# Half of g's blocks back to TensorE for tiles 4 to 9 of a fused attention, MoE and soft-MoE kernel

## The chip, the cores and the metric

One core of a Trainium2 chip runs the whole program. The metric is the device time of one execution in microseconds, the median of several; lower is better. The kernel before takes 519.07 us (3 runs, 516.73 to 519.13).

## The reference

Three layers follow each other, all in float32. The first is attention for 4 batches and 8 heads of width 64: 512 local queries see a band of 32 positions to either side and the 32 global keys, and 32 global queries see everything. The second is a dense layer pair with a leaky ReLU. The third is a soft mixture of experts with 8 experts of 4 slots.

```python
out_g = softmax(scale * q_g @ k_all.T) @ v_all
out_l = softmax([scale * q_l @ k_g.T, masked(scale * q_l @ k_l.T)]) @ [v_g, v_l]
x = concat([out_g, out_l])          # 4*544 rows of 512
h = x @ w_in                        # 512 -> 2048
g = maximum(0.01 * h, h)
x = g @ w_out                       # 2048 -> 512
logits = x @ phi                    # 512 -> 32 slots
d = softmax over rows(logits);  c = softmax over slots(logits)
slot_input = d.T @ x
slot_out[e] = maximum(slot_input[e] @ w1[e], 0) @ w2[e]
out = c @ slot_out
```

## The kernel before, in words

The 2176 rows of x are worked in 17 tiles of 128 rows (`NTT`): tiles 0 to 15 are the local queries of four batches, four tiles each, and tile 16 the global queries. The product with `w_out` is never formed per row: `pmat` holds `w_out @ phi`, so the logits come straight from g, and the product `d.T @ g` (`b_U`, into `uacc`) is multiplied by `w_out` once at the end.

For each tile t the work has two halves.

- **H(t)**, in `b_H`: for each of four blocks f of 512 features, 12 matmuls (`hp`, line 684) form h on TensorE, and ScalarE evicts them with the leaky ReLU to g (line 691).
- **L(t)**: g is needed with its features on the partitions to be multiplied by `pmat` (`b_M`, `lg`, line 735). There are two ways to turn it. In `b_L`, TensorE transposes four 128x128 blocks into a PSUM bank (`gtp`, line 721), and ScalarE or VectorE copies the bank to `gT` (line 723). In `blocks`, VectorE turns every 32x32 block in place (`gb`, line 703), and 16 copies per pair of f, of 32 partitions by 256 elements, move the blocks to their place (`g8`, line 712). The table `MOVE` says who copies: for f = 0 and 1 GpSimd alone, for f = 2 and 3 six copies on GpSimd, five on VectorE, five on ScalarE.

The logits then go through the softmax over rows, in running form: `b_D1` copies them out (`lp`, line 744), `b_D2` sums the four parts on TensorE (line 750), takes the maximum (line 754) and the exponentials (`st`, line 759, and the copy of line 760), `b_D3` transposes them back (line 795) and copies `d` (line 782), and `b_U` multiplies `d` with g (`up`, line 805) and adds to `uacc` (line 810).

`BLK` names the tiles that take the way through `blocks`: tiles 4 to 14. Tiles 0 to 3 and the last two take `b_L`.

The attention of batches 2 and 3 is recorded between the tiles: `merge` lays its steps (`a_T`: transposes of k and q, `kTp` and `qTp`, evicted by ScalarE to `kT` and `qT`; `a_S`: scores `sc`, mask and maximum `se` on VectorE, exponentials on ScalarE; `a_E`: transposes `etp`, evicted to `eT`; `a_V`: `po`) beside the items of `b_items`. All transposes of the attention and of `b_L` share two PSUM banks, `tp`.

Two things set the order on an engine. A scheduler places the recorded instructions by their order in the program and by their dependences. And `behind` wraps an item in `tc.issue_after(ms["b"])`: its TensorE instructions may not stand ahead of the last matmul of the chain of L. In `b_items`, for a tile of `BLK` the halves 4 to 7 of H(t) stand behind the chain of L(t-1) in this way; for other tiles there is no such edge.

Past line 643 a line of the changed kernel has a number higher by one.

Of the kernel before, what the change touches and what calls it, by code (L numbers as in the profile page):

```python
# [20 lines left out]
def kernel(  # L21
# [26 lines left out]
    NTT = B * NT + 1  # L48
# [13 lines left out]
    def tp(name):  # L62
        return bank("tp", name, 2)

    def hb(name):
        return bank("hb", name, 2)
# [149 lines left out]
    def part(name, dt=F32):  # L216

        if not spare:
            t = sb.tile([P, 2, 512], dt, tag="gT", name=name, bufs=2)
            spare.extend((t[:, 1], t[:, 0]))  # L220
        return spare.pop()
# [418 lines left out]
    gt = {}  # L640
    ms = {}
    seq = [(b, T) for b in range(B) for T in range(NT)] + [None]
    BLK = range(4, NTT - 2)
    MOVE = "P" * 16, "PPPPPPDDDDDAAAAA"
    gp = []

    def b_X(t):
        if seq[t] is None:
            pt = xg0.rearrange("p k t -> p (k t)")
        else:  # L650
            b, T = seq[t]
            pt = tp("xtp")
            for i in range(KD):
                nc.tensor.transpose(
                    pt[:, P * i:P * i + P],
                    xn[b][:, T, 2 * i:2 * i + 2, :].rearrange("p h d -> p (h d)"), ident,
                )
        pool, tags = (sa, ("qn", "kn")) if t == 2 else (sb, ("xh", "xl"))
        xh, xl = (pool.tile([P, KD, P], F32R, tag=g, name="x" + g, bufs=2) for g in tags)
        nc.scalar.mul(xh.rearrange("p k t -> p (k t)"), pt, WS)  # L660
        nc.vector.scalar_tensor_tensor(
            out=xl.rearrange("p k t -> p (k t)"), in0=pt, scalar=WS,
            in1=xh.rearrange("p k t -> p (k t)"), op0=ALU.mult, op1=ALU.subtract,
        )
        xt[t] = (xh, xl)
# [3 lines left out]
    def b_H(t, f, half=None):  # L669
        xh, xl = xt[t]  # L670
        if half != 1:
            if f == 0:
                gt[t] = (
                    xa.tile([P, FF], F32, tag="xn", name="gx", bufs=1) if t in (3, NTT - 1)
                    else sa.tile([P, FF], F32, tag="vw", name="g2", bufs=2) if t == 2
                    else sb.tile([P, FF], F32, tag="g", name="g", bufs=2)
                )
            hps[0] = hb("hp")
        hp = hps[0]
        w = wi[f]  # L680
        lo, hi = {None: (0, KD), 0: (0, KD // 2), 1: (KD // 2, KD)}[half]
        for k in range(lo, hi):
            for n, (a, c) in enumerate(((xh, 0), (xh, 1), (xl, 0))):
                nc.tensor.matmul(  # L684
                    hp, a[:, k, :], w[c][:, k, :],
                    start=(k == 0 and n == 0), stop=(k == KD - 1 and n == 2),
                )
        if half == 0:
            return
        gs = gt[t][:, 512 * f:512 * f + 512]  # L690
        nc.scalar.activation(out=gs, in_=hp, func=AF.Prelu, alpha=0.01)  # L691
        if t in BLK:
            blocks(t, f, gs)

    gbl = {}
# [1 line left out]
    def blocks(t, f, gs):  # L697

        if f % 2 == 0:
            gbl[0] = sb.tile([P, 2, 512], F32, tag="gT", name="gb", bufs=2)  # L700
            gbl[1] = gp[0].tile([P, 2, 4, P], F32, tag="g8", name="g8", bufs=2)
        gb, g8 = gbl[0], gbl[1]
        nc.vector.transpose(out=gb[:, f % 2], in_=gs)  # L703
        lst[t, f] = g8[:, f % 2]
        if f % 2 == 0:
            return
        src = gb.rearrange("p f (q c j) -> p (f q) c j", c=4, j=32)
        dst = g8.rearrange("p f q (a j) -> p (f q) a j", j=32)
        for n in range(16):
            a, c = n // 4, (n + n // 4) % 4  # L710
            copy = {"P": nc.gpsimd.tensor_copy, "A": nc.scalar.copy, "D": nc.vector.tensor_copy}[MOVE[f // 2][n]]
            copy(dst[32 * c:32 * c + 32, :, a], src[32 * a:32 * a + 32, :, c])  # L712
# [3 lines left out]
    def b_L(t, f, ev=None):  # L716
        g = gt[t]
        pt = tp("gtp")
        for c in range(4):
            o = 512 * f + P * c  # L720
            nc.tensor.transpose(pt[:, P * c:P * c + P], g[:, o:o + P], ident)  # L721
        gT = part("gT")
        (ev or (nc.vector.tensor_copy if f % 2 and not (t >= 6 and f in (1, 3, 9)) else nc.scalar.copy))(
            gT, pt
        )
        lst[t, f] = gT.rearrange("p (c t) -> p c t", c=4)

    def b_M(t, fs=range(NQ)):
        if 0 in fs:
            ms["M"] = bank("sm", "lg", 1)  # L730
        lg = ms["M"]
        for f in fs:
            gT = lst.pop((t, f))
            for c in range(4):
                ms["b"] = nc.tensor.matmul(  # L735
                    lg[32 * c:32 * c + 32, 0:P], pmat[:, c, f, :], gT[:, c, :],
                    start=(f == 0), stop=(f == NQ - 1), skip_group_check=True,
                ).ins
        return lg

    def b_D1(t):
        lg = b_M(t, range(2, NQ) if t in BLK else range(NQ))
        lp = sb.tile([P, 2 * P], F32, tag="lp", name="lp", bufs=1)[:, 0:P]
        nc.vector.tensor_copy(lp, lg[:, 0:P])
        ms["lg"] = lg, lp
# [28 lines left out]
    def b_D2(t):  # L774
        lg, lp = ms["lg"]
        ms["st"] = d_cols(lg[:, P:2 * P], lp)
        ms["b"] = ms["mm"]
# [15 lines left out]
    def b_D3(t):  # L793
        lg, _ = ms["lg"]
        ms["b"] = nc.tensor.transpose(lg[:, 256:384], ms["st"], ident).ins
        ms["d"] = d_rows(t, lg[:, 256:320])
# [19 lines left out]
    def b_U(t):  # L816
        u_add([(ms["d"], gt.pop(t))], t)
# [44 lines left out]

    def l_items(t):
        return ([(0.0, lambda: None), (0.6, lambda: b_M(t, range(2)))] if t in BLK else [
            (0.9, lambda: (b_L(t, 0), b_L(t, 1))),
            (0.9, lambda: (b_L(t, 2), b_L(t, 3))),
        ]) + [
            (1.3, lambda: b_D1(t)),
            (0.3, lambda: b_D2(t)),
            (0.1, lambda: b_D3(t)),  # L870
            (1.0, lambda: b_U(t)),
        ]

    def h_items(t):
        its = [(2.6, lambda f=f: b_H(t, f)) for f in range(NQ)]
        if t + 1 < NTT:
            its.insert(2, (0.5, lambda: b_X(t + 1), t + 1))
        return its

    def behind(item):  # L880
        def go():
            with tc.issue_after(ms["b"]):
                item[1]()
        return (item[0], go) + item[2:]

    def b_items(t0, t1):
        its = []
        for t in range(t0, t1):
            li = l_items(t - 1)
            h = [(1.3, lambda t=t, f=f, a=a: b_H(t, f, a)) for f in range(NQ) for a in range(2)]  # L890
            x = [(0.5, lambda t=t: b_X(t + 1), t + 1)] if t + 1 < NTT else []
            if t - 1 in BLK:
                its += h[0:2] + [li[1]] + h[2:4] + [li[2]] + x + [behind(h[4])]
                its += [li[3]] + [behind(x) for x in h[5:8]] + [li[4], li[5]]
                continue
            its += h[0:2] + [li[0]] + h[2:4] + [li[1]] + h[4:5] + x + h[5:6]
            its += [li[2], h[6], li[3], h[7], li[4], (0.0, lambda: None), li[5]]
        return its
# [19 lines left out]
    t = wp.tile([P, 4, NT, 2, D], F32, tag="w", name="qk")  # L918
# [29 lines left out]
    for t in range(3):  # L948
        b_X(t)
        b_H(t, 0)  # L950
# [28 lines left out]
    for x in l_items(2):  # L979
        x[1]()  # L980
    load_v(NP + 1)
    l0, l1 = l_items(0), l_items(1)
    merge(l0 + h3[2:] + l1, s4[-1:] + s5 + s6 + s7)
    b_X(NT)
# [342 lines left out]
```

## Time and profile before

| What | Value |
|---|---|
| median of 3 runs | 519.07 us |
| the profiled execution, its own time | 516.28 us |
| its span in the profile | 514.2 us |
| mean granted clock of TensorE | 0.962 |
| TensorE busy with matmuls | 464.5 us (90%) |
| VectorE busy | 301.2 us (59%) |
| ScalarE busy | 248.7 us (48%) |
| GpSimd busy | 181.1 us (35%) |

The span is what the instructions cover; the time has what lies around it too. Busy shares are means over stages with different limits. The weights are converted and the attention of batches 0 and 1 runs until about 205 us; tiles 4 to 9 pass through L from there to about 360 us; tiles 10 to 16 follow until 450 us, and the experts, whose weights stream in, end the program.

### The profile page before, as it was taken

To read this page: it belongs to the slowest core of one execution; us is meant where nothing else is said; L and a number is where in the kernel's file an instruction comes from. 1 tells how busy PE (TensorE), PEld (TensorE's weight loads), DVE (VectorE), ACT (ScalarE), POOL (GpSimd) and SP (SyncE) were. 2 spreads that over 40 slices of the span, in tenths; PEclk is the share of its full clock that TensorE was granted. 3 is DMA by queue.
4 is the path that set the end of the run, shared out by engine and by line. 5 is a ranking of instruction groups with operands and counts; after the bars stand their busy time and mean duration, and the time that the engine had idled before them with its cause. 6 is when DMAs were issued, how large, how long until landed. Compare 5 with 4: busy or idle time off the path is not lost.

```text
span 514.2 us, 13727 instructions
## 1 busy us (share of the span) xinstructions
PE 464.5 (90%) x5279; PEld 322.2 (63%) x5279; DVE 301.2 (59%) x996; ACT 248.7 (48%) x762; POOL 181.1 (35%) x345
## 2 busy tenths in 40 slices
PE   8976988978999989689898899999999999999994
PEld 5644766556775657456675667677777777633353
DVE  4586769759576663866766975656555541312422
ACT  4787878759654163444525473144433442300222
POOL 2066688443202015206263636516656620000000
PEclk9978899979998999879999999999999999999998
DMA  9998767799755750602480500229620059999987
GB/s 178 235 231 229 212 216 297 209 303 275 189 116 107 169 114 1 131 8 56 127 149 9 108 8 0 84 83 399 256 83 2 0 196 342 385 378 377 302 249 207
DMA packets 122397, 90.25 MB, mean 176 GB/s; under 512 B 75804, under 2 KB 101212, under 8 KB 122332
## 3 DMA queue, kind: packets, MB, share of 16 engines
q1 hardware_dynamic: 119660, 88.33, 60.2%
q10 hardware_dynamic: 2672, 1.05, 0.8%
q8 instruction: 41, 0.67, 0.6%
q14 instruction: 24, 0.20, 0.1%
HBM read 76.68 MB, written 8.65 MB: 166 GB/s over the span
## 4 chain that ended last, share of the span: by engine, by line
PE 60%; DVE 13%; ACT 7%; DMA 5%; issue 3%; POOL 2%; SPq 0%; ACTq 0%; POOLq 0%; DVEq 0%
PE hp L684 29%; PE ehp L1167 3%; PE up L805 3%; PE lg L735 3%; ACT se L452 2%; PE gtp L721 2%; PE sc L432 2%; DMA rraw<-in_moe_w_out_dram 2%; DVE se L444 2%; DMA rraw<-in_moe_w_in_dram 2%; PE po L489 2%; PE sop L1243 1%; POOL wn L259 1%; PE etp L471 1%; PE sop L1221 1%
## 5 line engine op out<-in xcount | busy, mean ns | idle before, releaser
L684 PE MATMUL hp<-wi,xxh 128*128 128x512 f32 x512 | 166.5, 407 | 7.1 <-ACT g L691 3.6
L712 POOL COPY g<-gb 32x256 f32<-32x256 f32 x242 | 97.6, 403 | 95.8 <-DVE gb L703 37.5
L684 PEld LDWEIGHTS hp<-wi,xxh 128*128 128x128 f32 x512 | 92.8, 191 | 41.2 <-issue 12.0
L684 PE MATMUL hp<-wi,xxl 128*128 128x512 f32 x256 | 101.5, 397 | 0.0
L452 ACT ACTIVATE se<-se,nmx 128x128 f32<-128x128 f32 x128 | 49.6, 390 | 24.2 <-DVE nmx L450 21.4
L691 ACT ACTIVATE g<-hp 128x512 f32<-128x512 f32 x60 | 35.7, 594 | 47.6 <-PE hp L684 46.9
L684 PEld LDWEIGHTS hp<-wi,xxl 128*128 128x128 f32 x256 | 48.7, 190 | 12.1 <-issue 0.8
L703 DVE STREAM_TRANSPOSE gb<-g 128x512 f32<-128x512 f32 x44 | 30.9, 706 | 19.4 <-ACT g L691 19.0
L200 POOL COPY vw<-vw 32x1664 f32<-32x1664 f32 x10 | 15.7, 1574 | 70.1 <-DMA vw<-in_v_g_dram 39.2
L259 POOL TENSOR_TENSOR wn<-wn,rraw 128x256 int32<-128x256 int32 x32 | 26.3, 836 | 32.6 <-DMA rraw<-in_moe_w_in_dram 23.4
L432 PE MATMUL sc<-kw,qT 64*32 64x128 f32 x1024 | 29.3, 292 | 1.1 <-issue 0.7
L444 DVE CUSTOM_DVE_ANT_0 se<-sc,mask 128x128 f32<-128x128 f32 x128 | 28.7, 282 | 1.4 <-PE sc L432 1.2
L471 PE MATMUL etp<-identr,se 128*128 128x128 f32 x128 | 23.1, 301 | 5.3 <-ACT kT L392 4.0
L259 POOL TENSOR_TENSOR wo<-wo,rraw 128x256 int32<-128x256 int32 x23 | 18.1, 800 | 25.5 <-DMA rraw<-in_moe_w_out_dram 4.5
L712 ACT COPY g<-gb 32x256 f32<-32x256 f32 x55 | 22.1, 402 | 9.2 <-DVE cs L788 4.1
L489 PE MATMUL po<-vw,eT 128*32 128x64 f32 x1024 | 24.0, 227 | 2.4 <-DMA vw<-vw 1.5
L249 ACT ACTIVATE rraw<-rraw 128x256 int32<-128x256 uint32 x55 | 23.2, 435 | 5.9 <-DMA rraw<-in_moe_w_in_dram 5.1
L432 PEld LDWEIGHTS sc<-kw,qT 64*32 64x32 f32 x1024 | 20.2, 112 | 7.7 <-issue 4.0
L403 DVE COPY kw<-kT 128x672 f32<-128x672 f32 x32 | 19.2, 638 | 9.0 <-ACT kT L392 8.8
L759 ACT ACTIVATE st<-lg,nm 128x128 f32<-128x128 f32 (+1 forms) x16 | 6.0, 373 | 38.2 <-DVE nm L758 34.5
L489 PEld LDWEIGHTS po<-vw,eT 128*32 128x32 f32 x1024 | 18.4, 113 | 9.7 <-issue 7.3
L452 ACT ACTIVATION_READ_ACCUMULATOR se<-se,nmx 128x1 f32 x128 | 24.1, 188 | 0.0
(227 smaller groups left out, 818.1 us busy)
## 6 DMA issues: line engine op xcount, KB each, us to landing
ew<-in_moe_w_dram SPq DMA_DIRECT2D x23, 1024.0 KB, 8.6
rraw<-in_moe_w_in_dram SPq DMA_DIRECT2D x32, 256.0 KB, 3.6
vw<-in_v_l_dram SPq DMA_DIRECT2D x60, 112.0 KB, 3.5
rraw<-in_moe_w_out_dram SPq DMA_DIRECT2D x23, 256.0 KB, 5.3
ew<-in_moe_w_dram SPq DMA_DIRECT2D x9, 512.0 KB, 9.6
ew<-in_moe_w_dram SPq DMA_DIRECT2D x17, 256.0 KB, 5.6
wo_f<-wo SPq DMA_DIRECT2D x16, 256.0 KB, 3.4
vn<-in_v_l_dram SPq DMA_DIRECT2D x4, 1024.0 KB, 6.1
```

The source lines that it names most:

```text
L249: nc.scalar.activation(out=m, in_=lo, func=AF.Copy, scale=2.0 ** -29)
L259: nc.gpsimd.tensor_tensor(out=di, in0=di, in1=m, op=ALU.add)
L403: nc.vector.tensor_copy(kw[:, :, 0:96], src)
L432: nc.tensor.matmul(bks[e][32 * u:32 * u + 32, P * T:P * T + P], qt[64 * e:64 * e + 64, 32 * U:32 * U + 32], kw[win(U) // (NW // 2)][64 * e ...
L444: nc.vector.tensor_tensor_reduce(out=s[:, T, :], in0=bk[:, P * T:P * T + P], in1=mask[:, 0 if T == 0 else 2 if T == NT - 1 else 1, :], sca ...
L452: exp_last[0] = nc.scalar.activation(out=s[:, T, :], in_=s[:, T, :], func=AF.Exp, bias=nmx[:, e, T:T + 1], accum_out=sm[:, T, e:e + 1],).ins
L471: nc.tensor.transpose(pt[:, P * T:P * T + P], es[e][:, T, :], ident)
L489: nc.tensor.matmul(pov[32 * u:32 * u + 32, T, e, :], ets[e][:, 32 * U:32 * U + 32], vw[:, win(U), e, :], start=True, stop=True,)
L684: nc.tensor.matmul(hp, a[:, k, :], w[c][:, k, :], start=(k == 0 and n == 0), stop=(k == KD - 1 and n == 2),)
L691: nc.scalar.activation(out=gs, in_=hp, func=AF.Prelu, alpha=0.01)
L703: nc.vector.transpose(out=gb[:, f % 2], in_=gs)
L712: copy(dst[32 * c:32 * c + 32, :, a], src[32 * a:32 * a + 32, :, c])
```

## The change

Tiles 4 to 9 leave `BLK` and form `HALF`. For them only f = 0 and 1 go through `blocks`; f = 2 and 3 go through `b_L`. The items of L get no `behind` in `b_items`, since that is done for `BLK` only, and all 16 matmuls of `b_M` are recorded in `b_D1`.

```diff
-    BLK = range(4, NTT - 2)
+    BLK = range(10, NTT - 2)
+    HALF = range(4, 10)
...
         nc.scalar.activation(out=gs, in_=hp, func=AF.Prelu, alpha=0.01)
-        if t in BLK:
+        if t in BLK or t in HALF and f < 2:
             blocks(t, f, gs)
...
         return ([(0.0, lambda: None), (0.6, lambda: b_M(t, range(2)))] if t in BLK else [
-            (0.9, lambda: (b_L(t, 0), b_L(t, 1))),
+            (0.0, lambda: None) if t in HALF else (0.9, lambda: (b_L(t, 0), b_L(t, 1))),
             (0.9, lambda: (b_L(t, 2), b_L(t, 3))),
         ]) + [
```

How this moves instructions is shown at three places. The first is TensorE, where the chain of tile 3 ends and that of tile 4 begins (kTp and qTp are the attention's transposes of k and q, etp those of its exponentials). Before:

```order
L735 MATMUL lg<-gT,pmat 32x128 x8
L471 MATMUL etp<-identr,se 128x128 x8
L750 MATMUL lg<-lp,s_77 128x128
L388 MATMUL kTp<-identr,kn 128x128 x4
L388 MATMUL qTp<-identr,qn 128x128 x4
L471 MATMUL etp<-identr,se 128x128 x4
```

And now:

```order
L736 MATMUL lg<-gT,pmat 32x128 x8
L471 MATMUL etp<-identr,se 128x128 x8
L751 MATMUL lg<-lp,s_77 128x128
L388 MATMUL kTp<-identr,kn 128x128 x4
L388 MATMUL qTp<-identr,qn 128x128 x4
L722 MATMUL gtp<-identr,g 128x128 x4
L796 MATMUL lg<-identr,st 128x128
```

The transposes of g stand where those of the exponentials stood, and the transpose of `st` follows at once; the etp of this step come later.

The second place is ScalarE in the same stretch, around the eviction of `kT` (se are the exponentials of the attention). Before:

```order
L660 ACTIVATE xxh<-xtp 128x512
L712 COPY g_3180<-gb 32x8x32 x2
L452 ACTIVATE se,sm<-se,nmx 128x128 x4
L712 COPY g_3180<-gb 32x8x32 x3
L452 ACTIVATE se,sm<-se,nmx 128x128 x4
L392 ACTIVATE kT<-kTp 128x512
L759 ACTIVATE st,zt<-lg,nm 128x128
L392 ACTIVATE qT<-qTp 128x512
```

And now:

```order
L661 ACTIVATE xxh<-xtp 128x512
L452 ACTIVATE se,sm<-se,nmx 128x128 x4
L392 ACTIVATE kT<-kTp 128x512
L452 ACTIVATE se,sm<-se,nmx 128x128 x4
L760 ACTIVATE st,zt<-lg,nm 128x128
L392 ACTIVATE qT<-qTp 128x512
```

The five block copies are gone, and `kT` is evicted after four exponentials, not eight.

The third place is TensorE between the sum of tile 4's logits (`b_D2`) and the transpose of its `st` (`b_D3`). Before, with 18 matmuls of `hp` among them:

```order
L750 MATMUL lg<-lp,s_77 128x128
L684 MATMUL hp<-wi,xxh 128x512 x2
L684 MATMUL hp<-wi,xxl 128x512
L521 MATMUL gg<-kgT,qgT 32x32 x8
...
L489 MATMUL po<-vw,eT 32x64 x8
L388 MATMUL kTp<-identr,kn 128x128 x4
L388 MATMUL qTp<-identr,qn 128x128 x4
L489 MATMUL po<-vw,eT 32x64 x23
L795 MATMUL lg<-identr,st 128x128
```

And now:

```order
L751 MATMUL lg<-lp,s_77 128x128
L489 MATMUL po<-vw,eT 32x64 x14
L388 MATMUL kTp<-identr,kn 128x128 x4
L489 MATMUL po<-vw,eT 32x64 x15
L388 MATMUL qTp<-identr,qn 128x128 x4
L796 MATMUL lg<-identr,st 128x128
```

No `hp` stands between the two any more; they stand ahead of line 751.

## Rows read from the trace of the kernel before

**Rows 1.** Busy time by stage: engine, busy us, instructions; then granted clock, DMA.

```profile
205.00:262.00 57.00, 48.48 (x793) 33.60 (x795) 39.75 (x141) 26.79 (x94) 18.02 (x39) 0.91 0.36 83
262.00:300.00 38.00, 34.41 (x526) 24.59 (x523) 28.13 (x109) 18.64 (x71) 18.99 (x34) 1.00 0.43 77
300.00:360.00 60.00, 58.80 (x571) 43.15 (x570) 36.82 (x101) 24.59 (x68) 28.62 (x72) 1.00 0.34 122
```

**Rows 2.** Waits of PE, 205 to 262 us: us in total, times, longest.

```profile
PE up L805 <- DVE d L782: 1.6, 1, 1.6
```

**Rows 3.** Waits of PE, 262 to 360 us.

```profile
PE hp L684 <- DVE uacc L810: 1.2, 1, 1.2
PE kTp L388 <- DVE eT L473: 1.1, 1, 1.1
```

**Rows 4.** Chain that ended last: start us, us, what (x58: two rows per matmul).

```profile
206.61 0.59 PE gtp L721 x4
...
229.79 0.84 PE po L489 x58
...
425.20 0.44 PE gtp L721 x4
```

**Rows 5.** Instructions on tile gtp: count, duration ns min/median/max.

```profile
L721 PE MATMUL gtp<-identr,g x64: 270/272/330, 135.7 to 440.9; 128*128 128x128 f32 x64
L723 ACT COPY gT<-gtp x16: 563/586/588, 140.5 to 442.4; 128x512 f32<-128x512 f32 x16
```

**Rows 6.** Groups by line, 205 to 360 us: count, busy us, mean ns, idle before.

```profile
L703 DVE STREAM_TRANSPOSE gb<-g 128x512 f32<-128x512 f32 x27 | 18.9, 705 | 7.9 <-ACT g L691 7.5 <-ACT al L764 0.3
...
L712 DVE COPY g<-gb 32x256 f32<-32x256 f32 x35 | 14.9, 426 | 0.6
L712 ACT COPY g<-gb 32x256 f32<-32x256 f32 x35 | 14.1, 402 | 6.3 <-DVE nmx L450 3.9 <-DVE cs L788 2.0
```

**Rows 7.** Busy time in stretches of 2 us; columns of rows 1.

```profile
216.00:218.00 2.00, 0.00 (x0) 0.00 (x0) 1.93 (x6) 1.95 (x8) 1.77 (x6) 0.50 0.72 164
...
224.00:226.00 2.00, 2.00 (x10) 0.24 (x9) 1.99 (x19) 0.00 (x0) 0.00 (x0) 0.50 0.00 0
```

**Rows 8.** ScalarE in order of time: start us, us, what, idle before.

```profile
213.95 0.81 ACT L712 COPY g<-gb 32x256 f32<-32x256 f32 x2 [3.91 <-DVE nmx L450]
...
216.44 1.23 ACT L712 COPY g<-gb 32x256 f32<-32x256 f32 x3
...
219.23 0.57 ACT L392 ACTIVATE kT<-kTp 128x512 f32<-128x512 f32 x1
```

**Rows 9.** VectorE in order of time.

```profile
212.37 0.71 DVE L703 STREAM_TRANSPOSE gb<-g 128x512 f32<-128x512 f32 x1
...
239.96 0.28 DVE L760 COPY st<-lg 32x128 f32<-32x128 f32 x1 [0.23 <-ACT st L759]
...
242.82 1.33 DVE L703 STREAM_TRANSPOSE gb<-g 128x512 f32<-128x512 f32 x2
...
246.05 1.57 DVE L712 COPY g<-gb 32x256 f32<-32x256 f32 x4
...
271.88 3.19 DVE L712 COPY g<-gb 32x256 f32<-32x256 f32 x5
...
277.00 0.74 DVE L810 SCALAR_TENSOR_TENSOR uacc<-uacc,al,up 128x512 f32<-128x512 f32 x1
```

**Rows 10.** TensorE in order of time.

```profile
219.86 1.11 PE L471 MATMUL etp<-identr,se 128*128 128x128 f32 x4 [4.05 <-ACT kT L392]
...
226.22 0.73 PE L684 MATMUL hp<-wi,xxh 128*128 128x512 f32 x2
...
237.73 0.49 PE L750 MATMUL lg<-lp,s 128*128 128x128 f32 x2
...
244.89 0.33 PE L795 MATMUL lg<-identr,st 128*128 128x128 f32 x1
...
248.80 1.06 PE L805 MATMUL up<-g,d 128*32 128x512 f32 x8 [1.62 <-DVE d L782]
```

## The prediction

> **What bounds the kernel now.** I read the busy time by stage first. TensorE is the engine to follow: from 205 to 262 us it is busy 48.48 of 57 us, from 262 to 300 us 34.41 of 38, from 300 to 360 us 58.80 of 60 [rows 1]. VectorE comes next, 39.75 of 57 and 28.13 of 38 us in the first two stretches and 36.82 of 60 in the third; ScalarE is lower in each. So the 155 us in which tiles 4 to 9 pass through L are three stages with different limits. In the last one TensorE has 1.2 us to spare, and any work added there lengthens the program. In the first two it idles 8.5 and 3.6 us, 12.1 together.
>
> Next the waits of TensorE, to see who ends that idle time. Nearly all of it stands behind ScalarE and VectorE: 4.05 us for the eviction of kT [rows 10], 1.6 for `d` [rows 2], 1.2 for `uacc`, 1.1 for `eT` [rows 3]. These are in-order queues, so I looked in the order of time at what stands in them just before. Ahead of kT, ScalarE makes five block copies, two and three, 2.04 us in all [rows 8]; ahead of the same exponentials VectorE turns blocks twice, the first of the two for 0.71 us [rows 9]. Ahead of `d` stand two turns of 1.33 us and four copies of 1.57 us, ahead of `uacc` five copies that took 3.19 us [rows 9]. This is work that the change removes.
>
> The clock last: TensorE's granted clock is 0.50, the lower of its two levels, from 216 to 226 us, five rows in a line of which the first and the last are shown [rows 7]. Before it fell, TensorE had been idle or nearly so; from 219.86 us on it worked at that clock until matmuls of `hp` began at 226.22 [rows 10]. About 6.1 us of work ran at half speed, so some 3.1 us were lost on top of the idle time.
>
> **What it adds.** Six tiles times two blocks times four transposes: 48 transposes on TensorE, in 12 groups. The chain shows a group of four at 0.59 us, and at 0.44 where it follows long matmuls [rows 4]. I take 0.59, since the start of the next group of long matmuls then pays the difference. Of the 12 groups the first, tile 4's f = 2, stands in the new order right behind qTp, in the hole of 4.05 us [rows 10], and costs nothing as long as some hole is left there. The other eleven cost 11 x 0.59 = **6.5 us**. The lower bound is 11 x 0.44 = 4.8; the upper is a whole transpose each time, 48 x 0.272 = 13.1 us [rows 5], if none overlapped the next.
>
> The trace can be set against a rule here. The Trainium skill, page "TensorE: Matmul & The Clock Gate", section "Part 4: PE-mode transpose", gives about 275 ns for a 128x128 transpose inside a kernel; that is of bf16, and by it the 48 would cost 13.2 us. The single durations agree with it, 0.272 us [rows 5], but four in a row take 0.59 and not 1.1 us [rows 4], so I use the chain and keep the other price as a rival.
>
> The bank of each group has to be evicted: 12 copies of about 0.586 us [rows 5], two on VectorE (f = 3 of tiles 4 and 5), ten on ScalarE. They lie beside TensorE's work.
>
> **What it takes away.** Per tile VectorE loses two turns of 0.705 and five copies of 0.426, together 3.5 us, and ScalarE five copies of 0.402, 2.0 us [rows 6], against one or two evictions. GpSimd loses six copies. None of that is on the path by itself; it counts where TensorE waited behind it:
>
> - The hole at 219.86 us. Without the two turns VectorE reaches the negated maxima about 1.2 us sooner, so the exponentials start near 212.7. In the new order ScalarE does four of them (it needs 1.7 us for four, from the end of the first two copies to the next three), then kT, then four, then `st`: kT is done by about 215 where it starts at 219.23 now [rows 8]. TensorE then does the first group and waits for `st`, which I place at 217 to 218. It goes on some 1.9 us sooner than at 219.86. The etp and half of the scores of this step come after `hp` now and run at full clock if it is back by then; the work from 219.86 to 226.22 took 6.4 us [rows 10], and the part that is moved would save up to 1.3. I take 1.9 and half of that: **2.6 us**. Bounds: nothing, if kT was not what held it, and 4.05 + 3.1 = 7.1, if the hole and the low clock both go.
> - The wait for `d`, 1.62 us [rows 10]: 2.9 us of turns and copies are gone from the queue ahead of it. But in the new order only 29 matmuls of `po` and eight transposes stand between lines 750 and 795 for tile 4, 0.84 us and two groups of 0.59, about 2.0 us [rows 4], where 7.2 us lay between them before, 237.73 to 244.89 [rows 10]. The chain in between, maximum, exponential and copy, took until 240.24, 2.5 us [rows 9, 10]. So some 0.4 come back: **1.2 us**, between 0 and 1.6.
> - The wait for `uacc`, 1.18 us: the five copies ahead of it are gone: **1.2 us**, between 0 and 1.2.
> - The wait for `eT`, 1.07 us, follows from the same late queue by way of the exponentials. Half of it: **0.5 us**.
> - All else that TensorE idles from 205 to 360 us is 13.3 - 4.05 - 1.62 - 1.18 - 1.07 = 5.4 us, in small pieces. A tenth: **0.5 us**.
>
> The edges cost little by themselves: from 300 us on, where most of them act, TensorE idles 1.2 us in 60. Taking them away gives nothing there, and six groups (3.5 us) are added to that stage.
>
> **The sum.** 6.5 - 2.6 - 1.2 - 1.2 - 0.5 - 0.5 = +0.5 us. It is made against the profiled execution, 516.28 us, which lies 2.8 us under the median; against the median it is 519.07 + 0.5 = **519.5 us**. What shifts at 360 us shifts to the end, since from there to 440 us TensorE is busy without a hole and the experts' weights wait for buffers that its matmuls free.
>
> **The rivals.**
>
> *Slower: the freed time turns into new waits.* Without the edges nothing keeps `hp` between the links of the softmax chain. For tile 4 no `hp` is left between lines 750 and 795, tile 6 has 17 `po`, four etp and eight transposes of k and q there, tile 9 two long matmuls and eight transposes, as the new order stands. On ScalarE the global queries' exponentials of tile 4's stretch stand ahead of `st` now. Each link that is not covered costs what the chain needs beyond its cover, some 0.4 us as worked out for tile 4 and up to 2.5 if nothing covers it. If the six tiles pay 1 us each, the 6 us saved are gone, and the time is 519.07 + 6.5 = **525.6 us**. It decides from 2.1 us of new waits on, about 0.35 per tile. For it: VectorE stays the second busiest in the first two stages, and the two banks of `tp` get 12 more users. Against it: VectorE loses 3.5 us a tile.
>
> *Slower by the price of a transpose.* If each group stood alone, waiting for a bank, and paid 0.272 us four times, 13.1 - 6.0 = +7.1: **526.2 us**. It is the page's price named above as a mechanism of this kernel; the 0.59 us of the chain speak against it.
>
> *Faster: the holes close and the clock stays up.* If TensorE gets enough to do between 213 and 220 us for the clock not to fall, 7.1 us come back there instead of 2.6, and with 1.6, 1.2, 1.1 and half of the small pieces, 2.7, the saving is 13.7: 519.07 + 6.5 - 13.7 = **511.9 us**. With the clock falling as before but the holes closed (4.05 + 1.6 + 1.2 + 1.1 + 2.7 = 10.7) it is 514.9. For it: every large wait stands behind work that goes, and the new order has etp, scores and `hp` mixed more finely. Against it: with kT early, the next link, `st`, is late by nearly as much.
>
> **How the numbers follow.** A measurement of this kernel can tell about 0.5%, 2.6 us, from no change. Saving and cost nearly cancel, and each is uncertain by 3 us or more. I give the forecast, within 2.6 us of 519.07, 0.36; its own range is 516.5 to 521.7. The slower cases get 0.32 (0.27 new waits, 0.05 the full price), the faster ones 0.32. The range reaches to 512.5 below, near the second faster case and short of the whole of the first, and to 526.5 above, which holds both slower cases as worked out; outside it lies what both ends would add to each other.
>
> **What the profile after would show.** Right: 12 new groups of `gtp` from 205 to 365 us at 0.44 to 0.59 us in the chain; kT evicted near 215 us; TensorE's idle time from 205 to 360 us down from 13.3 to between 6 and 9 us; waits for `uacc` and `d` under 0.5 us; the stage from 300 us longer by about 3.5 us. Wrong to the slow side: waits of line 795 or of `up` for `st` or `d` in most of tiles 4 to 9, or waits of transposes for a bank. Wrong to the fast side: no row at clock 0.50 around 220 us.

## The result and the profile after

The changed kernel takes 521.40 us (median of 20 runs, 517.06 to 524.57) where the kernel before, timed beside it, takes 517.92 us (20 runs, 514.30 to 521.56). The ratio is 1.006, 95% interval [1.0038, 1.0082]: slower by about 3.1 us, where the forecast was +0.5. Timed a second time (the seventh experiment) the same kernel stood at 1.0021 [0.9988, 1.0054]. So its loss is between nothing and 4 us, and it lies at the edge of what a measurement of this kernel can tell; a loss of 2.0 to 2.8 us lies in both intervals.

The head of the profile page after; its own time is 521.22 us:

```profile
span 519.1 us, 13708 instructions
...
PE 473.6 (91%) x5327; PEld 326.3 (63%) x5327; DVE 282.1 (54%) x956; ACT 240.7 (46%) x742; POOL 165.7 (32%) x309
```

VectorE, ScalarE and GpSimd lost 19, 8 and 15 us of work, and TensorE gained 9. The busy time by stage, columns as in [rows 1]:

```profile
205.00:262.00 57.00, 53.54 (x725) 35.97 (x723) 30.81 (x106) 19.72 (x68) 14.90 (x33) 0.94 0.40 85
262.00:300.00 38.00, 37.49 (x489) 26.77 (x485) 18.86 (x84) 16.64 (x58) 13.36 (x28) 1.00 0.25 55
300.00:360.00 60.00, 58.45 (x711) 43.14 (x711) 30.22 (x104) 23.59 (x77) 23.21 (x53) 1.00 0.29 90
```

TensorE idled 8.5, 3.6 and 1.2 us in these stretches before; it idles 3.5, 0.5 and 1.6 us now, 5.5 in place of 13.3. What is left are these waits of TensorE from 205 to 365 us (us in total, times, longest):

```profile
PE lg L796 <- DVE st L761: 1.9, 1, 1.9
PE gtp L722 <- ACT gs L538: 1.6, 1, 1.6
PE lg L751 <- DMA vw<-in_v_l_dram: 0.9, 1, 0.9
...
PE gtp L722 <- ACT kT L392: 0.3, 1, 0.3
```

Those for `d`, `uacc` and `eT` [rows 2, 3] are gone, but for 0.3 us or less. The wait for `gs` is one for a bank: ScalarE, in making `gs`, empties one of the two banks of `tp` that the transposes share. The place of the largest, TensorE in order of time:

```profile
215.63 0.49 PE L751 MATMUL lg<-lp,s 128*128 128x128 f32 x2 [0.93 <-DMA vw<-in_v_l_dram]
...
217.87 1.11 PE L722 MATMUL gtp<-identr,g 128*128 128x128 f32 x4 [0.32 <-ACT kT L392]
220.88 0.47 PE L796 MATMUL lg<-identr,st 128*128 128x128 f32 x1 [1.89 <-DVE st L761]
...
222.70 1.93 PE L806 MATMUL up<-gx,d 128*32 128x512 f32 x8
```

and ScalarE there:

```profile
217.24 0.57 ACT L392 ACTIVATE kT<-kTp 128x512 f32<-128x512 f32 x1
```

The hole of 4.05 us [rows 10] has become one of 0.3 and one of 1.9 with a group of `gtp` between. The clock still falls, for a shorter time: 218 to 225 us, where it was 216 to 226 before [rows 7]. The first and the last of four rows in a line (the row ahead of them has 0.96):

```profile
218.00:220.00 2.00, 0.98 (x4) 0.58 (x4) 2.00 (x3) 2.00 (x11) 1.17 (x1) 0.50 0.86 196
...
224.00:226.00 2.00, 2.00 (x10) 1.23 (x7) 1.30 (x3) 0.00 (x0) 0.00 (x0) 0.84 0.00 0
```

So the holes, the idle times of TensorE, closed as forecast, and yet the kernel is not faster. To see where the gain went I measured one stretch in all the profiles: from the sum of tile 3's logits (line 750, now 751) to that of tile 10. Up to its start the profiled executions differ by themselves (it lies at 213.30 us before, at 215.63 after and between 210.6 and 217.0 over all profiles). TensorE's matmuls stand in the same order before and after until then, and the first `hp` already starts at 51.3 us before and at 53.8 after. From the end of the stretch on each execution takes 150.2 to 151.7 us, so comparing this stretch leaves most of that spread out. Before, in one row of the busy time by stretch:

```profile
213.30:364.01 150.71, 138.93 (x1757) 99.51 (x1758) 100.39 (x326) 68.06 (x227) 66.44 (x148) 0.97 0.37 102
```

and after:

```profile
215.63:368.51 152.88, 147.89 (x1806) 104.47 (x1806) 80.99 (x287) 60.09 (x207) 50.01 (x109) 0.98 0.35 96
```

TensorE's idle time falls by 11.8 - 5.0 = 6.8 us, and its busy time rises by 9.0. Counted in the trace from one matmul's start to the next, with gaps over 0.1 us as idle, that is:

| us in the stretch | before | after | edges back (eighth experiment) | order back, no edges (sixth) |
|---|---|---|---|---|
| idle | 11.8 | 4.9 | 5.4 | 3.9 |
| the 48 `gtp` | 0 | 6.3 | 6.1 | 6.3 |
| all other matmuls | 138.9 | 141.7 | 137.2 | 137.5 |
| of that, lost at the lower clock (estimate) | 3.1 | 1.9 | 1.5 | 1.7 |
| all other matmuls without that loss | 135.8 | 139.8 | 135.7 | 135.8 |
| of all other matmuls, the 318 `hp` | 77.2 | 78.7 | 77.6 | 78.2 |
| unbroken runs of `hp` | 29 | 37 | 32 | 32 |

What is lost at the lower clock is estimated as half of the time that these matmuls took while the granted clock was 0.50. The transposes cost 6.3 us, 0.52 a group, and the idle time that went pays for them. The last part of the loss was not in the forecast: the same other matmuls, in the same number, take 2.8 us longer, though less is lost to the clock. Without the clock's part they take 4.0 us longer. The last two columns are experiments of the next section, and show what this part comes from.

### The profile page after: what moved, and what is told of

Its sections match the earlier page's. It is cut to its first block, busy times and chain, and to the rows that moved or that the text cites. A ratio compares the mean times of both kernels' runs of the same rounds, so it can differ in the third digit from the quotient of the medians.

```text
span 519.1 us, 13708 instructions
## 1 busy us (share of the span) xinstructions
PE 473.6 (91%) x5327; PEld 326.3 (63%) x5327; DVE 282.1 (54%) x956; ACT 240.7 (46%) x742; POOL 165.7 (32%) x309
## 4 chain that ended last, share of the span: by engine, by line
PE 65%; DVE 8%; DMA 7%; ACT 6%; issue 2%; POOL 2%; SPq 0%; ACTq 0%; POOLq 0%; DVEq 0%
PE hp L685 30%; PE up L806 3%; PE ehp L1168 3%; PE sc L432 3%; PE po L489 3%; PE lg L736 3%; PE gtp L722 2%; DMA rraw<-in_moe_w_in_dram 2%; DMA rraw<-in_moe_w_out_dram 2%; PE etp L471 2%; PE sop L1244 1%; PE sop L1222 1%; POOL wn L259 1%; PE op L1268 1%; DVE se L444 1%
## 5 line engine op out<-in xcount | busy, mean ns | idle before, releaser
L713 POOL COPY g<-gb 32x256 f32<-32x256 f32 x206 | 82.1, 399 | 76.6 <-DVE gb L704 63.9
L704 DVE STREAM_TRANSPOSE gb<-g 128x512 f32<-128x512 f32 x32 | 22.3, 705 | 25.1 <-ACT g L692 19.8
L432 PE MATMUL sc<-kw,qT 64*32 64x128 f32 x1024 | 31.2, 294 | 0.5 <-DVE kw L403 0.5
L473 DVE COPY eT<-etp 128x512 f32<-128x512 f32 x28 | 18.8, 687 | 7.2 <-PE etp L471 6.9
L497 DVE TENSOR_TENSOR xn<-po,rs 128x512 f32<-128x512 f32 x16 | 11.0, 687 | 19.1 <-PE po L489 17.2
```

The costliest lines, as they stand in the source:

```text
L432: nc.tensor.matmul(bks[e][32 * u:32 * u + 32, P * T:P * T + P], qt[64 * e:64 * e + 64, 32 * U:32 * U + 32], kw[win(U) // (NW // 2)][64 * e ...
```

## The experiments

In all of them the outputs are computed in full. Ratios are to the kernel before in the same set of runs: 516.08 us for the first four, 515.71 for the next four and 516.72 for the last four. The ratio and the quotient of the two medians are not the same estimate, and where they differ by much both are given. The theories have the letters that the expectations give them.

**The edges alone, on the changed kernel.** The items of L of tiles 4 to 9 are recorded as for `BLK` again, with `behind`:

```diff
-            if t - 1 in BLK:
+            if t - 1 in BLK or t - 1 in HALF:
```

> The changed kernel with the order edges put back for tiles 4 to 9, so that only the way of turning g differs from the kernel before. Theory A (work against holes): each group of four transposes costs about 0.52 us of TensorE, 6.3 us in all, and is paid for only as far as holes of TensorE close; the edges matter little. Expect 2 to 4 us over the kernel before, as the changed kernel. Theory B (order): the transposes are paid by the holes, and the loss comes from the missing edges, which let TensorE change more often between kinds of matmuls. Expect the time of the kernel before or 1 to 3 us under it.

Measured: 516.14 us, 1.001 [0.9968, 1.0051]. The loss is gone, as theory B has it, but no gain appears. Theory A had 2 to 4 us over the kernel before.

**The edges alone, on the kernel before.** Tiles 4 to 9 turned by VectorE in full, recorded as the change records them:

```diff
-            if t - 1 in BLK:
+            if t - 1 in BLK and t - 1 >= 10:
```

> The kernel before with the order edges taken away for tiles 4 to 9, all of g still turned on VectorE. Theory A: within 1 us of the kernel before. Theory B: about 3 us slower.

Measured: 543.4 us, 1.0505 [1.0454, 1.0555]. Both theories missed this by far. For the old way of turning g the edges with their order are worth 27 us. Its waits of TensorE from 205 to 365 us show how the time goes; the idle time in the stretch is 25 us, not 12:

```profile
PE kTp L388 <- DVE eT L473: 4.6, 2, 3.9
PE xtp L654 <- ACT kT L392: 4.1, 1, 4.1
PE lg L795 <- DVE st L760: 2.9, 1, 2.9
PE up L805 <- DVE d L782: 1.8, 3, 1.2
PE etp L471 <- ACT qT L392: 1.7, 1, 1.7
```

**Half of the tiles.** The change for tiles 4 to 6 alone, then for 7 to 9 alone (`BLK` holds the others):

```diff
-    HALF = range(4, 10)
+    HALF = range(4, 7)
```

> The change for tiles 4 to 6 alone; tiles 7 to 9 stay on VectorE with their edges. Theory A: 24 transposes cost 3.1 us, but these are the tiles whose stage has the holes (11 us of the 12 that TensorE idles between the two marks), so nearly all that the change recovered (6.9 us) comes back: 0 to 4 us faster than the kernel before. Theory B: half of the edges are gone, so half of the loss, 1 to 2 us slower.

Measured: 518.47 us, 1.0042 [1.0013, 1.007].

```diff
-    HALF = range(4, 10)
+    HALF = range(7, 10)
```

> The change for tiles 7 to 9 alone. Theory A: 3.1 us of transposes in a stage in which TensorE idles 1.2 us in 60: 2.5 to 4 us slower than the kernel before. Theory B: half of the edges are gone, 1 to 2 us slower.

Measured: 521.96 us, 1.0108 [1.0066, 1.0149]. Neither half gains by itself, and the tiles that come later lose more. Theory A had a gain for the first half, which did not come. For the second it had 2.5 to 4 us of loss and theory B 1 to 2, and 5.6 were measured. The stretch of the fourth kernel is 5.9 us longer than before: 3.0 by the transposes, 1.7 by idle time and, as estimated, 1.9 by the lower clock, with 0.7 less on other matmuls.

**Edges and the first three tiles.** The first and the third edit together:

```diff
+    BLK = range(7, NTT - 2)
+    HALF = range(4, 7)
...
+            if t - 1 in BLK or t - 1 in HALF:
```

> The change with the order edges kept, for tiles 4 to 6 alone. Theory C (so far: a group of transposes costs 0.5 us, holes of TensorE pay for it only where there are any, before 300 us, and without the edges TensorE does the same work some 3 us slower): 24 transposes cost 3.0 us, most of the 6.2 us of holes that the version with edges for tiles 4 to 9 closed lies in these tiles: 1 to 3 us faster than the kernel before. Rival D (the closed holes come from tiles 7 to 9 too, or the freed engines only move the holes): within 1 us of the kernel before.

Measured: 511.03 us (507.86 to 514.94), 0.9925 [0.9894, 0.9955]. This beats both kernels, the one before by 3.9 us by the ratio and 4.7 by the medians, where theory C had 1 to 3. Its stretch:

```profile
212.87:358.12 145.25, 139.33 (x1781) 101.72 (x1782) 92.27 (x308) 62.85 (x216) 58.66 (x130) 0.99 0.41 114
```

TensorE idles 5.9 us in it; six groups of `gtp` have been added and the large holes are closed.

**The order without the edges.** `behind` is one thing, and the order in which the items are recorded another: for `BLK` the links of L stand behind halves 4, 5 and 8 of H, otherwise behind 6, 7 and 8, so that the logits' sum comes late and the links close together. The transposes of g, too, stand behind half 2 in the order of `BLK` and behind half 4 otherwise. Here tiles 4 to 9 are recorded in the order of `BLK` with no edge:

```diff
+            if t - 1 in HALF:
+                its += h[0:2] + [li[1]] + h[2:4] + [li[2]] + x + [h[4]]
+                its += [li[3]] + h[5:8] + [li[4], li[5]]
+                continue
```

> The changed kernel with its items recorded in the order that the edges go with (line 751 after the fourth half of H, and so on) but without the edges themselves. Separates the order of recording from the edges. If the edges do it: 2 to 4 us over the kernel before, as the changed kernel. If the order of recording does it: within 1 us of the kernel before.

Measured: 512.48 us, 0.9937 [0.9908, 0.9966], 3.2 us under the kernel before where at most 1 was expected. Its stretch, with the matmuls of the changed kernel:

```profile
215.90:363.70 147.80, 143.95 (x1805) 104.27 (x1805) 79.55 (x286) 60.46 (x207) 49.88 (x109) 0.99 0.36 100
```

**Two repeats**, the changed kernel and the first experiment, on the chip of the last two:

> The changed kernel beside the others on one chip: 2 to 4 us over the kernel before.

Measured: 517.62 us, 1.0021 [0.9988, 1.0054], which is 1.1 us over the kernel before by the ratio and 1.9 by the medians, under the 2 to 4 expected.

> The changed kernel with the order edges put back, beside the changed kernel on one chip. Theory C: within 1 us of the kernel before and 2 to 4 us under the changed kernel. If the first measurement was chance: as the changed kernel.

Measured: 515.73 us, 1.0008 [0.9987, 1.003]. It is level with the kernel before as expected, but only 1.9 us under the changed kernel by the medians, just short of the 2 to 4 expected, and the two intervals overlap, so this repeat alone does not show that order and edges together bring the loss back. On one chip, then, the changed kernel takes 517.62 us and with the one order put back 512.48, and here the intervals do not meet. The edit that costs is the order of recording. The edges are not missed once TensorE turns half of g, and with them on all six tiles the time lies between: TensorE then waits 2.0 and 0.7 us for evictions of `gT` (the eighth kernel, 205 to 365 us):

```profile
PE lg L796 <- DVE st L761: 2.1, 1, 2.1
PE etp L471 <- ACT gT L724: 2.0, 1, 2.0
...
PE lg L736 <- ACT gT L724: 0.7, 1, 0.7
```

Whether these waits make the 3.2 us between the sixth and the eighth is not shown: the stretch takes 147.2 and 148.8 us with the edges (first and eighth) and 147.8 without them.

**Halves of the tiles in that order.** As the sixth, with `HALF` as in the third and the fourth:

> Turned half by TensorE for tiles 4 to 6 alone, recorded in the order of the edges but without edges for them. Theory C (transposes at 0.5 us a group against holes that lie before 300 us; the order of recording makes the rest of the difference): 12 groups fewer than with tiles 4 to 9, which ran 3.2 us under the kernel before, and their 3 us had few holes to go into: 4 to 6 us under the kernel before. Rival D (tiles 7 to 9 paid for themselves): about 3 us under it.

Measured: 514.18 us, 0.9926 [0.9889, 0.9962], under the kernel before by 3.8 us by the ratio and 2.5 by the medians. That is too near both numbers to tell theory C from D. With edges (the fifth) the ratio is the same, within intervals of 0.4% to either side.

> The same for tiles 7 to 9 alone. Theory C: 12 groups, 3 us, against 1.2 us of holes in their stage: 1 to 3 us over the kernel before. Rival D: level or faster.

Measured: 525.54 us, 1.0123 [1.0068, 1.0177]. Theory C had 1 to 3 us of loss here, so it missed; it is 6.4 by the ratio and 8.8 by the medians. The waits of TensorE in the stretch tell why:

```profile
PE lg L751 <- DVE lp L745: 5.2, 2, 3.7
PE etp L471 <- ACT kT L392: 4.0, 1, 4.0
PE up L806 <- DVE d L783: 1.9, 2, 1.6
...
PE hp L685 <- DVE uacc L811: 1.2, 1, 1.2
```

The holes of tiles 4 to 6 are all there, as before [rows 2, 3, 10], and a new one of 3.67 us stands at 294 us:

```profile
294.30 0.49 PE L751 MATMUL lg<-lp,s 128*128 128x128 f32 x2 [3.67 <-DVE lp L745]
```

`lp` there is tile 6's, which VectorE still turns in full, and the clock is at 0.74 and then 0.50 in the four microseconds from 294 us on. The fourth kernel has the same wait, 3.67 us, without the order edit. So tiles 7 to 9 lose by what happens at the seam between the two ways of turning, besides the price of their own transposes. The stretch is 6.4 us longer than before: 2.9 by the transposes, 1.5 by idle time, 0.6 by the clock, and 1.4 by the other matmuls without the clock's part.

**Twice the transposes.** As the sixth, with all four f of tiles 4 to 9 turned by TensorE, 96 transposes in place of 48 and no block copies:

> The price of the transposes doubled: for tiles 4 to 9 all four blocks of g are turned by TensorE (96 transposes), in the same order of recording, without edges. Theory C: 24 groups where there were 12, 6.3 us more, and only some 4 us of idle time left to take them: 4 to 6 us over the version with half, so 1 to 3 us over the kernel before. Rival D (the holes still pay): level with the version with half, 3 us under the kernel before.

Measured: 517.67 us, 1.0004 [0.9971, 1.0038], 0.67% or 3.5 us over the sixth by the ratios. Theory C had 4 to 6, and rival D, level with the sixth, is refuted. The gain of the sixth is gone, though 3.5 us is less than the 6.3 that twelve more groups take at 0.52 each. It is not the price of the groups alone: the order of the matmuls differs too, and `hp` stands in 37 runs in this stretch where it stands in 32 in the sixth. How the 3.5 us divide is not shown.

**The order on the kernel before.** Tiles 4 to 9 turned by VectorE, in the order of `BLK`, with no edge:

```diff
+            if 4 <= t - 1 < 10:
+                its += h[0:2] + [li[1]] + h[2:4] + [li[2]] + x + [h[4]]
+                its += [li[3]] + h[5:8] + [li[4], li[5]]
+                continue
```

> The kernel before without the edges for tiles 4 to 9 but with its order of recording kept, all of g on VectorE. If the 27 us that taking edges and order away together cost came from the order of recording: within 3 us of the kernel before. If the edges hold the order there: 15 us or more slower.

Measured: 545.54 us, 1.054 [1.0493, 1.0586]. Here the order does not help: where VectorE turns all of g, it is the edges that hold the schedule together. The second experiment's 27 us are theirs.

## Why the prediction was right and wrong

**The cost of the transposes** was right. 6.5 us were forecast for eleven groups, and 6.3 were measured for all twelve, 0.6 of it by the lower clock. Pieces of the chain after, of two groups, of one and of two again (start us, us, what):

```profile
257.83 0.88 PE gtp L722 x8
...
327.71 0.59 PE gtp L722 x4
...
349.59 1.03 PE gtp L722 x8
```

The rival with the full price of 0.272 us four times is refuted. The Trainium skill, page "TensorE: Matmul & The Clock Gate", section "Part 4: PE-mode transpose", has about 275 ns for one transpose, of bf16. A single one here agrees (median 273 ns); an estimate from the page's figure gives 13.2 us for the 48, and the measured 6.3 decides for what they take one behind another.

**What it takes away** came out somewhat larger: 6.0 us were forecast, 5.3 of them idle time and 0.7 the clock, and 6.9 us of idle time and some 1.2 us of the clock went. The hole at kT went as forecast. On the scale of the kernel before, 2.33 us earlier by the starts of the stretch, the eviction of kT starts at 214.9 us and ends at 215.5 (forecast: done by about 215), and the transpose of `st` starts at 218.6 (forecast 217 to 218) and waited for `st`, the link named as late next. The waits for `d` and `uacc` went, and the small pieces gave more than a tenth: 5.5 us of idle time from 205 to 360 us is under the 6 to 9 forecast. The clock was low for a shorter time. The prediction had TensorE "idle or nearly so" before the clock fell in the kernel before; the busy time by 2 us has it at work 0.49 us from 212 to 214 us and 1.25 us from 214 to 216. That the stage from 300 us would be 3.5 us longer can't be read, since the new order moves work across its borders; TensorE idles 1.6 us in it, as much as before within 0.4.

**New waits**, the slower rival with 0.27, did not come as described. It needed 2.1 us of waits of `up` or line 795 over the six tiles. There is one of 1.9 us, which the forecast itself contains. Of its other sign, waits of transposes for a bank, there is one of 1.6 us, for `gs`, and none before any other of the twelve groups but 0.3 us at the first.

**The step that failed** is "The edges cost little by themselves ... Taking them away gives nothing there", together with a term that is missing: what the other order of recording costs. The edit removes edges and order in one. Taking the edges alone away gains 3.2 us by the medians (the sixth against the eighth), but the order costs: 517.62 against 512.48 us on one chip, 5 us by the medians and 4 by the ratios. I looked for its price in waits, and most of it is in busy time. Against the sixth kernel, with as many matmuls, the changed one idles 1.0 us more and spends 141.7 - 137.5 = 4.2 us more on the others, 0.2 of them by the clock (1.9 - 1.7). The repeats agree: without the clock's part the others take 139.8 and 139.9 us in the two profiles of the changed kernel, and 135.9, 135.7 and 135.8 in the first, eighth and sixth.

Against the kernel before the terms of the stretch are +6.3 for the transposes, -6.9 for idle time, -1.2 for the clock and +4.0 for the other matmuls, together +2.2, which is the difference of the two stretches (152.88 - 150.71). The first three are what I had summed to +0.5; they come to -1.8. So that the time came out within 3 us of the forecast is in part luck: a sum that was 2.3 us too dear hid over half of a term of 4.0 that it lacked.

What makes the same matmuls longer is seen in the rows, though no run isolates one cause. The changed order cuts long runs into short ones. Pieces of its chain:

```profile
236.21 1.00 PE gl L515 x10
237.21 0.59 PE etp L471 x4
237.80 0.99 PE gl L515 x6
...
253.87 1.58 PE hp L685 x6
...
256.26 1.57 PE hp L685 x6
...
296.10 2.96 PE hp L685 x12
```

and of the sixth kernel's:

```profile
236.46 1.02 PE gl L515 x16
```

`gl` in two pieces takes twice what it takes in one, and two runs of six `hp` take 3.15 us where one of twelve takes 2.96. Without the clock's part `hp` goes with the number of its runs in the profiles of the other experiments too: 75.6 us with 23 runs (the twelfth), 76.6 with 26 (the second), 77.2 with 29 (before, fifth, ninth), 77.5 to 77.9 with 32, and 78.6 with 37 (the changed kernel, twice), some 0.2 us a run. That is 1.4 of the 4.0 us; `lg` has 1.1, `gl` 1.0, `sc` 0.9 and `po` 0.5, and other kinds give some 0.9 back. What each cut costs for these stays open.

The price of the order lies in tiles 4 to 6. With them alone the other matmuls take 139.7 us in the changed order and 135.2 in the order of `BLK` (third and ninth, without the clock's part). With tiles 7 to 9 alone it is the other way, 135.1 and 137.1 (fourth and tenth).

**Where the gain lies** was taken as a whole, and it is not even. Tiles 4 to 6 give all of it once the order of `BLK` is kept: 0.9925 and 0.9926. Tiles 7 to 9 with edges give it back (the eighth against the fifth, 1.0008 against 0.9925), and in the order without edges they add nothing that the intervals can tell (0.9937 against 0.9926). The forecast had said that the stage from 300 us has 1.2 us to spare; to leave tiles 7 to 9 as they were is what the fifth and the ninth kernel do.

Open is why the changed kernel stood at 1.006 in one comparison and 1.0021 in the other, and why its profiled executions reach the stretch 2 to 4 us later than that of before, though TensorE's order up to there is the same. Neither was tried.

## What to carry to other kernels

Price an added operation stage by stage against the idle time of that stage, and apply the change to the tiles whose stage has holes. Where an edit changes a branch that also sets the order in which work is issued, cost the order as a term of its own, and look for its price in busy time as well as in waits.

## What the runs showed that was not expected

- Four f32 transposes of 128x128 take 0.52 us on average where a single one lasts 0.273.
- The edges, without which the kernel before takes 5.0 to 5.4% longer, are worth nothing measurable once half of each tile's turning leaves VectorE and the same order is kept: 0.9925 with them and 0.9926 without for tiles 4 to 6, each within 0.4%. On all six tiles the kernel is 3.2 us faster without them, by the medians.
- The same matmuls in the same number took 141.7 us in the changed kernel and 137.2 in the eighth, by their order, with 0.4 us of that from the clock (1.9 - 1.5).
